# Cached decode attention, two branches: 20 of 128 token slots of each value tile weighted by ScalarE and summed by VectorE, outputs gathered two groups at a time

## The chip, the cores and the metric

The kernel runs on one core of one Trainium2 chip. The metric is the device time of one execution in microseconds (us); the verdict on a change is taken between runs of both kernels on the same chip.

## What is computed

Two attention branches A and B each answer one new token per batch entry (2 of them) against a cache of 4096 tokens, 32 heads, head size 128, all in float32. Their outputs are mixed by a gate:

```python
q = (x @ wq).reshape(B, 1, 32, 128).transpose(0, 2, 1, 3)
scores = einsum("bhqd,bhkd->bhqk", q, k_cache) * 128 ** -0.5
p = softmax(scores, axis=-1)
o = einsum("bhqk,bhkd->bhqd", p, v_cache)
branch = o.transpose(0, 2, 1, 3).reshape(B, 1, 4096) @ wo
g = sigmoid((A_x * gate_w).sum(-1, keepdims=True))
out = g * branch_A + (1 - g) * branch_B      # both branches are fed A_x
```

The four caches are 134.2 MB each (2 x 32 x 4096 x 128 x 4 bytes), the four weight matrices 8.4 MB each. Every byte is used once, so some 570 MB have to be read from HBM.

## The kernel before

The work is cut into 32 **units** (`units`, `NU`): branch n, group g of four heads, batch entry b. A unit's keys fill one tile `kt` of 128 partitions x 128 token slots x 128 values (8.4 MB), and its values one tile `vt` of the same size. Each of the four heads has a quarter of the partitions, 32 of them, and a partition holds 128 consecutive tokens, the **slots**. There are two key buffers (`kpool`, also used for `wq` and `wo`) and one value buffer (`vpool`).

All big loads go out on SyncE's one queue, in the order of a list written out by hand (`order`): wq of A, wq of B, the keys of unit 0, and then the keys of unit u+1 and the values of unit u, in turn; at the end wo of A, the values of unit 31 (three pieces) and wo of B (six pieces). `pump` issues the next load of the list once the buffer that it needs has been given free by `used`; on the chip SyncE waits at each load for the last reader of that buffer. So the values of unit u are issued after the last value product of unit u-1 (the buffer is the same one), and the keys of unit u+2 after the scores of unit u.

The schedule is manual: each engine runs its instructions as the program writes them. The loop over u (at the end of the function) handles the keys of unit u and the values of unit v = u-1 together:

- `scores(u, k)`, four chunks of 32 slots: VectorE multiplies the chunk in place by the query (L232, TENSOR_TENSOR) and sums each slot over its 128 values (L233, TENSOR_REDUCE into `sc`). Chunks 0 and 1 stand before `values(v)` in the program, chunks 2 and 3 behind it, but `values(v)` is work of TensorE alone.
- `values(v)`: 32 products (L258), each of four slots: the weights `padded` (128 x 32) against 128 x 512 of `vt`, into `vp` in PSUM. A product shows as two MATMUL records in the trace, 64 for a unit. GpSimd then clears the weights (L261).
- `take_out` and `gather_out`, every second unit, when both batch entries of a group are in: ScalarE (L275) and VectorE (L281, three times) fold the four slot columns of `vp` into `vs`, and a product with `pick` (L285) places them in `heads`.
- `soft(u)`: maximum over slots and partitions (L241, L244, L246 on VectorE), then ScalarE's four exponentials, one per head, straight into `padded` (L249), each with its row sum into `lp`.
- `sum_of(n)` and `deal_out(n)`, once per branch: the row sums become `rs`, and eight products with the table `deal` (L294) turn `heads` into `on`, the layout that the product with wo wants (`project_out`, L307, and `project_last`, L318).

## Time and profile before

| | |
|---|---|
| median of three runs | 1326.93 us (1326.4 to 1327.3) |
| the profiled execution | 1326.39 us |
| its span, first to last instruction | 1324.6 us |
| VectorE (DVE) busy | 1181.6 us, 89% |
| TensorE (PE) busy | 356.9 us, 27% |
| ScalarE (ACT) busy | 74.6 us, 6% |
| read from HBM | 570.43 MB, 431 GB/s over the span |

Busy times are shares of the whole span. In the rows below DVE is VectorE, PE TensorE, ACT ScalarE, SPq SyncE's queue. A row of a timeline has start and length in us; in brackets stand the idle time before it and what ended that.

### The profile page before, as it was taken

The numbers are of one execution on the slowest core, as the hardware profiler recorded it, in microseconds if no ns is written. First come the engines' busy times: TensorE is split into PE (matmuls) and PEld (weight loads), VectorE is DVE, ScalarE is ACT, GpSimd is POOL, SyncE is SP. The second block draws the span as 40 slices with busy tenths as digits, with TensorE's granted clock in tenths as the row PEclk, the third lists the DMA queues.
The fourth block names the chain that finished last, engine by engine and source line by source line (L and its number), as shares of the span: only waits on it lengthen the run. The fifth ranks groups of instructions, "written<-read, shape, count | busy, mean of one in ns | idle before, by whom it ended". The sixth has DMA issues, their size and how long they took to land.

```text
span 1324.6 us, 5989 instructions
## 1 busy us (share of the span) xinstructions
PE 356.9 (27%) x2406; PEld 104.7 (8%) x2406; DVE 1181.6 (89%) x477; ACT 74.6 (6%) x285; POOL 18.0 (1%) x40
## 2 busy tenths in 40 slices
PE   3202322211232221123233022232202222220257
PEld 0000000000000000000001000000000000000012
DVE  2499999999999999999999999999999999999960
ACT  0000000000000000000000000000000000000000
POOL 0000000000000000000000000000000000000000
PEclk9656666556666655666665566666556666656667
DMA  9999999999999999999999999999999999999998
GB/s 412 442 436 422 440 441 418 439 440 430 433 434 439 426 431 441 434 435 426 441 430 432 440 426 440 433 434 429 440 437 422 440 439 426 431 442 439 418 431 346
DMA packets 11130, 570.83 MB, mean 431 GB/s; under 512 B 1239, under 2 KB 1243, under 8 KB 1630
## 3 DMA queue, kind: packets, MB, share of 16 engines
q1 hardware_dynamic: 11092, 570.43, 99.5%
q8 instruction: 19, 0.31, 0.1%
q14 instruction: 9, 0.07, 0.0%
q10 hardware_dynamic: 10, 0.01, 0.0%
HBM read 570.43 MB, written 0.00 MB: 431 GB/s over the span
## 4 chain that ended last, share of the span: by engine, by line
DMA 76%; PE 23%; issue 0%; DVE 0%; SPq 0%; ACT 0%
DMA vt<-in_A_v_cache_dram 37%; DMA vt<-in_B_v_cache_dram 35%; PE vp L258 22%; DMA kt<-in_B_wq_dram 3%; DMA kt<-in_B_wo_dram 2%; PE qa L209 1%; DVE kt L215 0%; SPq L62 0%; ACT kt L214 0%; PE qa L318 0%; ACT kt L376 0%; DVE qcolB L217 0%
## 5 line engine op out<-in xcount | busy, mean ns | idle before, releaser
L232 DVE TENSOR_TENSOR kt<-kt,q 128x4096 f32<-128x4096 f32 x128 | 565.5, 4418 | 46.2 <-DMA kt<-in_B_k_cache_dram 28.9
L233 DVE TENSOR_REDUCE sc<-kt 128x32 f32<-128x4096 f32 x128 | 565.7, 4420 | 6.5
L258 PE MATMUL vp<-vt,pr 128*32 128x512 f32 x2048 | 298.9, 749 | 797.4 <-DMA vt<-in_A_v_cache_dram 424.2
L258 PEld LDWEIGHTS vp<-vt,pr 128*32 128x32 f32 x2048 | 81.8, 134 | 1005.2 <-issue 1000.5
L249 ACT ACTIVATE pr<-sc,nm 32x128 f32<-32x128 f32 x128 | 50.9, 398 | 723.7 <-DVE nm L246 721.3
L285 PE MATMUL heads<-vs,pick 128*128 128x128 f32 x32 | 12.4, 491 | 124.2 <-DVE vs L281 124.2
L261 POOL MEMSET pr<- 128x512 f32 x32 | 16.8, 524 | 1268.0 <-PE vp L258 1230.1
L275 ACT ACTIVATE vs<-vp,slot 128x128 f32<-128x128 f32 x16 | 5.9, 368 | 451.0 <-PE vp L258 451.0
L281 DVE SCALAR_TENSOR_TENSOR vs<-vp,slot,vs 128x128 f32<-128x128 f32 x48 | 16.7, 348 | 13.5 <-ACT vs L275 12.4
L209 PE MATMUL qa<-kt,cols 128*2 128x512 f32 x128 | 18.3, 728 | 22.1 <-DMA kt<-in_B_wq_dram 15.8
L249 ACT ACTIVATION_READ_ACCUMULATOR pr<-sc,nm 32x1 f32 x128 | 23.5, 184 | 0.0
L215 DVE STREAM_TRANSPOSE kt<-kt 128x1024 f32<-128x1024 f32 x1 | 1.2, 1245 | 21.8 <-ACT kt L214 21.8
L307 PE MATMUL most<-kt,on 128*2 128x512 f32 x120 | 17.3, 734 | 11.1 <-DMA kt<-in_A_wo_dram 10.7
L285 PEld LDWEIGHTS heads<-vs,pick 128*128 128x128 f32 x32 | 7.8, 304 | 138.8 <-DVE vs L281 138.8
L378 DVE COPY kt<-qa 2x128 f32<-2x128 f32 x2 | 0.6, 280 | 14.6 <-PE qa L318 14.6
L337 DVE TENSOR_REDUCE kt<-kt 128x32 f32<-128x128 f32 x1 | 0.4, 378 | 13.7 <-POOL kt masks.py:199 13.7
L215 DVE STREAM_TRANSPOSE vt<-vt 128x1024 f32<-128x1024 f32 x1 | 1.2, 1245 | 10.0 <-ACT vt L214 10.0
L241 DVE TENSOR_REDUCE rm<-sc 128x1 f32<-128x128 f32 x32 | 9.0, 281 | 0.6
L244 DVE STREAM_TRANSPOSE q<-rm 128x32 f32<-128x32 f32 x32 | 6.8, 211 | 1.1
L294 PE MATMUL small<-vs,deal 128*128 128x32 f32 x32 | 7.2, 402 | 0.9 <-ACT vs L290 0.9
L294 PEld LDWEIGHTS small<-vs,deal 128*128 128x128 f32 x32 | 7.0, 330 | 1.4 <-ACT vs L290 1.4
L146 DVE COPY cols<-small 128x8 f32<-128x8 f32 x1 | 0.2, 167 | 7.6 <-PE small L144 7.6
(53 smaller groups left out, 44.0 us busy)
## 6 DMA issues: line engine op xcount, KB each, us to landing
kt<-in_A_wq_dram SPq DMA_DIRECT2D x2, 4096.0 KB, 16.6
kt<-in_A_k_cache_dram SPq DMA_DIRECT2D x2, 4096.0 KB, 31.2
vt<-in_B_v_cache_dram SPq DMA_DIRECT2D x1, 4096.0 KB, 20.2
kt<-in_B_wo_dram SPq DMA_DIRECT2D x1, 4096.0 KB, 33.4
vt<-in_B_v_cache_dram SPq DMA_DIRECT2D x1, 3072.0 KB
kt<-in_B_wo_dram SPq DMA_DIRECT2D x1, 2048.0 KB
...
```

Source lines behind the costliest of these rows:

```text
L209: nc.tensor.matmul(t[h * QT:h * QT + B], cols[:, c], halves[:, c, i, h], start=c == 0, stop=c == KC - 1)
L232: nc.vector.tensor_tensor(t, t, qs[u][:, None, :].to_broadcast([P, NH, DH]), op=ALU.mult)
L233: nc.vector.tensor_reduce(sc[u][:, k * NH:(k + 1) * NH], t, axis=AX.X, op=ALU.add)
L241: nc.vector.tensor_reduce(rm, sc[u], axis=AX.X, op=ALU.max)
L244: nc.vector.transpose(across, rm.to_broadcast([P, PH]))
L249: nc.scalar.activation(padded[h, :, b, j * VC:(j + 1) * VC], sc[u][h].rearrange("p (c a) -> p c a", a=VC), AF.Exp, bias=nm[h], accum_out=l ...
L258: nc.tensor.matmul(vp[n, g][s * QT:(s + 1) * QT], padded[:, c].rearrange("p b m -> p (b m)"), vt[u][:, c * VC:(c + 1) * VC].rearrange("p a ...
L261: nc.gpsimd.memset(padded[:, :, b], 0.0)
L281: nc.vector.scalar_tensor_tensor(t, vp[n, g][:, a * DH:(a + 1) * DH], slot[:, a:a + 1], t, op0=ALU.mult, op1=ALU.add)
L285: nc.tensor.matmul(heads[n], pick[:, (NG - g) * B:][:, :P], t, start=g == 0, stop=g == NG - 1)
L294: nc.tensor.matmul(dealt[:, b], deal[:, b, k].rearrange("p g h q -> p (g h q)"), t[:, k * OR:(k + 1) * OR], start=k == 0, stop=k == DQ - 1)
L307: nc.tensor.matmul(most[s * QT:s * QT + B], on[n][:, r], wo[n][:, r], start=n == "A" and r < STRIPS, stop=n == "B" and r >= EARLY - STRIPS)
```

## The change

1. **Values.** Slots 0 to 19 of the value tile no longer go through five products. `weigh`: ScalarE multiplies each of the 20 slots by its probability, in place (20 ACTIVATEs of 128 x 128). `add_up`: VectorE adds the five blocks of four slots into the first with three TENSOR_TENSORs (1024, 512 and 512 elements per partition). `values_added`: one product with a constant table `plain` takes the sum. So a unit has 27 + 1 products in place of 32.
2. **Order.** `scores(u, 2)` moves between `values` and `add_up`, so on VectorE the three additions stand between the third and the fourth chunk. The value buffer is given free after `values_added`.
3. **Scores.** In chunk 0, the sums of 12 of the 32 slots go from VectorE to ScalarE (12 ACTIVATEs with an accumulated sum); VectorE's first reduction is left with 20 slots.
4. **Softmax.** One exponential over 128 partitions into `pc`, with its row sum into `ls`, then four copies into `padded` (27 blocks of 4 slots in place of 32).
5. **Outputs.** `vs` holds two groups; every fourth unit one product of 256 columns places both (`gather_out`). `sum_of` sums with two small products in place of a transpose and a reduction; `deal_out` turns the outputs with three VectorE transposes in place of eight products, and the table `deal` goes.
6. **Start.** wq of A is loaded by one DMA in place of two.

```diff
+ADDED = 5
+NA = ADDED * VC
+NP = NVC - ADDED
+HELP = 12
-        load(t, ins[n + "_wq"].rearrange("(p c) f -> p c f", c=KC), *((0, KC // 2, KC) if n == "A" else (0, KC)))
+        load(t, ins[n + "_wq"].rearrange("(p c) f -> p c f", c=KC), 0, KC)
...
     def scores(u, k):
...
-        nc.vector.tensor_reduce(sc[u][:, k * NH:(k + 1) * NH], t, axis=AX.X, op=ALU.add)
+
+        n = HELP if k == 0 else 0
+        for r in range(n):
+            nc.scalar.activation(t[:, r], t[:, r], AF.Copy, accum_out=sc[u][:, r:r + 1])
+        nc.vector.tensor_reduce(sc[u][:, k * NH + n:(k + 1) * NH], t[:, n:], axis=AX.X, op=ALU.add)
...
+        pc[u] = small.tile([P, NS], F32, name="pc")
+        nc.scalar.activation(pc[u], sc[u], AF.Exp, bias=nm, accum_out=ls[:, g % N2, g // N2, b:b + 1])
         for j, h in enumerate(QUARTERS):
-            nc.scalar.activation(padded[h, :, b, j * VC:(j + 1) * VC], sc[u][h].rearrange("p (c a) -> p c a", a=VC),
-                                 AF.Exp, bias=nm[h], accum_out=lp[h, g * B + b:g * B + b + 1])
+            nc.scalar.activation(padded[h, :, b, j * VC:(j + 1) * VC],
+                                 pc[u][h, NA:].rearrange("p (c a) -> p c a", a=VC), AF.Copy)
+
+    def weigh(u):
+
+        for r in range(NA):
+            nc.scalar.activation(vt[u][:, r], vt[u][:, r], AF.Copy, scale=pc[u][:, r:r + 1])
+
+    def add_up(u):
+
+        t = vt[u][:, :NA].rearrange("p (c a) d -> p c (a d)", a=VC)
+        nc.vector.tensor_tensor(t[:, 0:2], t[:, 0:2], t[:, 2:4], op=ALU.add)
+        nc.vector.tensor_tensor(t[:, 0], t[:, 0], t[:, 1], op=ALU.add)
+        nc.vector.tensor_tensor(t[:, 0], t[:, 0], t[:, 4], op=ALU.add)
...
-        for c in range(NVC):
...
+        for i in range(NP):
+            value_product(u, i, padded[:, i], NA + i * VC)
         nc.gpsimd.memset(padded[:, :, b], 0.0)
 
+    def values_added(u):
+        value_product(u, NP, plain[:, units[u][2]], 0)
...
+    def gather_out(n, y):
+
+        if y == 0:
+            heads[n] = ps.tile([P, N2, DH], F32, name="heads", bufs=1)
+        nc.tensor.matmul(heads[n].rearrange("p i d -> p (i d)"), pick[:, P - (y + 1) * QT:][:, :P],
+                         vs[n, y].rearrange("p i d -> p (i d)"), start=y == 0, stop=y == NG // N2 - 1)
...
+        for k in range(N2):
+            nc.scalar.activation(even[:, k], heads[n][:, k], AF.Copy, scale=rs[n][:, k:k + 1])
+
+        turned = small.tile([P, N2, DQ, QT], F32, name="turned")
+        nc.vector.transpose(turned.rearrange("p i q m -> p (i q m)"), even.rearrange("p i d -> p (i d)"))
+        on[n] = small.tile([P, B, OR], F32, name="on")
         for b in range(B):
-            for k in range(DQ):
-                nc.tensor.matmul(dealt[:, b], deal[:, b, k].rearrange("p g h q -> p (g h q)"), t[:, k * OR:(k + 1) * OR],
-                                 start=k == 0, stop=k == DQ - 1)
...
+            nc.vector.transpose(on[n][:, b], turned[:, :, :, :GB].rearrange("p i q (h b) -> p b i h q", b=B)[:, b])
...
         if v >= 0:
+            weigh(v)
             values(v)
+        if u < NU:
+            scores(u, 2)
+        if v >= 0:
+            add_up(v)
+            values_added(v)
             used("v", v)
         if ends:
             take_out(*ends)
         if u < NU:
-            scores(u, 2)
             scores(u, 3)
             used("k", u)
```

How the instructions stand now, at three places. In these rows a name is output<-inputs, `vt` a value tile, `kt` a key tile, and the brackets name the engines and loads whose count the instruction waits for.

VectorE in the loop's pass u = 1, before: the four chunks, each a multiplication and a reduction, and behind them the maximum.

```order
L232 TENSOR_TENSOR kt_210<-kt_210,q_237 128x4096 [waits DMAHW7_49,DVE_49,PE_49]
L233 TENSOR_REDUCE sc_239<-kt_210 128x32 [waits DVE_49,Activation_49]
L232 TENSOR_TENSOR kt_210<-kt_210,q_237 128x4096
L233 TENSOR_REDUCE sc_239<-kt_210 128x32 [waits DVE_49]
L232 TENSOR_TENSOR kt_210<-kt_210,q_237 128x4096
L233 TENSOR_REDUCE sc_239<-kt_210 128x32 [waits DVE_49]
L232 TENSOR_TENSOR kt_210<-kt_210,q_237 128x4096
L233 TENSOR_REDUCE sc_239<-kt_210 128x32 [waits DVE_49]
L241 TENSOR_REDUCE rm_286<-sc_239 128x1 [waits DVE_49]
```

The same pass now:

```order
L243 TENSOR_TENSOR kt_213<-kt_213,q_254 128x4096 [waits DMAHW6_49,DVE_49,PE_49]
L248 TENSOR_REDUCE sc_256<-kt_213 128x20 [waits DVE_49,Activation_49]
L243 TENSOR_TENSOR kt_213<-kt_213,q_254 128x4096
L248 TENSOR_REDUCE sc_256<-kt_213 128x32 [waits DVE_49]
L243 TENSOR_TENSOR kt_213<-kt_213,q_254 128x4096
L248 TENSOR_REDUCE sc_256<-kt_213 128x32 [waits DVE_49]
L277 TENSOR_TENSOR vt_215<-vt_215 128x1024 [waits DMAHW2_49,DMAHW7_49,DMAHW0_49,Activation_49]
L278 TENSOR_TENSOR vt_215<-vt_215 128x512 [waits DVE_49]
L279 TENSOR_TENSOR vt_215<-vt_215 128x512 [waits DVE_49,Activation_49]
L243 TENSOR_TENSOR kt_213<-kt_213,q_254 128x4096
L248 TENSOR_REDUCE sc_256<-kt_213 128x32 [waits DVE_49]
L256 TENSOR_REDUCE rm_334<-sc_256 128x1 [waits DVE_49]
```

The first reduction has shrunk to 20 slots, and three additions on the value tile, which wait for ScalarE, stand ahead of the fourth chunk. The first reduction of the pass before, u = 0, waits for nothing but VectorE:

```order
L243 TENSOR_TENSOR kt_169<-kt_169,q_217 128x4096 [waits DMAHW4_49,DMAHW1_49,DVE_49]
L248 TENSOR_REDUCE sc_219<-kt_169 128x20 [waits DVE_49]
L243 TENSOR_TENSOR kt_169<-kt_169,q_217 128x4096
L248 TENSOR_REDUCE sc_219<-kt_169 128x32 [waits DVE_49]
L243 TENSOR_TENSOR kt_169<-kt_169,q_217 128x4096 [waits DMAHW5_49]
```

TensorE at the end, before: the last unit's products, the gather, the eight products with `deal`, and the product with wo of B.

```order
L258 MATMUL vp<-vt,pr 32x512 [waits DMAHW0_49]
L258 MATMUL vp<-vt,pr 32x512 x3
L285 MATMUL heads<-vs,pick 128x128 [waits DVE_49]
L294 MATMUL small<-vs,deal 128x32 [waits Activation_49]
L294 MATMUL small<-vs,deal 128x32 x7
L307 MATMUL most<-kt,on 2x512 [waits DMAHW1_49,Activation_49]
```

And now:

```order
L285 MATMUL vp<-vt,pr 32x512 [waits DMAHW7_49]
L285 MATMUL vp<-vt,pr 32x512 x3
L285 MATMUL vp<-vt,plain 32x512 [waits DVE_49]
L327 MATMUL heads<-vs,pick 128x256 [waits DVE_49]
L350 MATMUL most<-kt,on 2x512 [waits DMAHW0_49,DVE_49]
```

The products with `deal` are gone; the product with wo waits for VectorE's transposes instead of ScalarE's copy.

## Rows read from the trace of the kernel before

**Rows 1.** The page: SyncE's DMA queue, packets, MB, share of 16 engines.
```profile
q1 hardware_dynamic: 11092, 570.43, 99.5%
```
**Rows 2.** The page: the chain that ended last, by engine.
```profile
DMA 76%; PE 23%; issue 0%; DVE 0%; SPq 0%; ACT 0%
```
**Rows 3.** Windows: stretch, length, busy (count) of PE, PEld, DVE, ACT, POOL; PEclk, DMA share, GB/s.
```profile
4.00:43.00 39.00, 11.96 (x78) 3.02 (x82) 8.91 (x31) 1.36 (x3) 0.00 (x0) 0.85 0.99 430
...
101.00:1262.00 1161.00, 295.25 (x1966) 87.75 (x1966) 1103.97 (x412) 64.77 (x257) 15.73 (x30) 0.61 1.00 434
```
**Rows 4.** The chain in order of time: start, length, what.
```profile
53.16 47.77 DMA vt<-in_A_v_cache_dram
...
101.07 9.80 PE vp L258 x64
110.89 28.66 DMA vt<-in_A_v_cache_dram
...
265.12 29.26 DMA vt<-in_A_v_cache_dram
...
1233.64 28.43 DMA vt<-in_B_v_cache_dram
...
1291.95 29.41 DMA kt<-in_B_wo_dram
...
1321.40 0.47 PE qa L318 x8
```
**Rows 5.** VectorE's timeline: first multiplication of passes 1, 2, 3 and 6.
```profile
89.37 4.43 DVE L232 TENSOR_TENSOR kt<-kt,q 128x4096 f32<-128x4096 f32 x1
...
125.85 4.43 DVE L232 TENSOR_TENSOR kt<-kt,q 128x4096 f32<-128x4096 f32 x1
...
163.23 4.42 DVE L232 TENSOR_TENSOR kt<-kt,q 128x4096 f32<-128x4096 f32 x1
...
275.18 4.43 DVE L232 TENSOR_TENSOR kt<-kt,q 128x4096 f32<-128x4096 f32 x1 [1.67 <-DMA kt<-in_A_k_cache_dram]
```
**Rows 6.** Groups by line and form, VectorE: xcount | busy us, mean ns | idle before, releasers.
```profile
L233 DVE TENSOR_REDUCE sc<-kt 128x32 f32<-128x4096 f32 x128 | 565.7, 4420 | 6.5
L232 DVE TENSOR_TENSOR kt<-kt,q 128x4096 f32<-128x4096 f32 x128 | 565.5, 4418 | 46.2 <-DMA kt<-in_B_k_cache_dram 28.9 <-DMA kt<-in_A_k_cache_dram 17.0
...
L223 DVE STREAM_TRANSPOSE q<-qcolB 128x128 f32<-128x128 f32 x16 | 5.0, 312 | 0.6
...
L148 DVE TENSOR_TENSOR vt<-cols,small 128x8 f32<-128x8 f32 x1 | 0.2, 168 | 0.0
```
**Rows 7.** The same of ScalarE.
```profile
L249 ACT ACTIVATE pr<-sc,nm 32x128 f32<-32x128 f32 x128 | 50.9, 398 | 723.7 <-DVE nm L246 721.3
L249 ACT ACTIVATION_READ_ACCUMULATOR pr<-sc,nm 32x1 f32 x128 | 23.5, 184 | 0.0
L275 ACT ACTIVATE vs<-vp,slot 128x128 f32<-128x128 f32 x16 | 5.9, 368 | 451.0 <-PE vp L258 451.0
```
**Rows 8.** Timeline of the start: issues of the first loads, the two query projections.
```profile
0.74 0.87 SPq L62 DMA_DIRECT2D kt<-in_A_wq_dram  x2
...
16.30 9.76 PE L209 MATMUL qa<-kt,cols 128*2 128x512 f32 x64 [6.22 <-DVE qa L205]
...
26.12 26.93 SPq L62 DMA_DIRECT2D kt<-in_A_k_cache_dram  x3
...
41.85 8.64 PE L209 MATMUL qa<-kt,cols 128*2 128x512 f32 x64 [15.78 <-DMA kt<-in_B_wq_dram]
```
**Rows 9.** TensorE's timeline at the end.
```profile
1307.32 0.49 PE L285 MATMUL heads<-vs,pick 128*128 128x128 f32 x2 [1.66 <-DVE vs L281]
1308.27 3.62 PE L294 MATMUL small<-vs,deal 128*128 128x32 f32 x16 [0.46 <-ACT vs L290]
1312.20 7.74 PE L307 MATMUL most<-kt,on 128*2 128x512 f32 x56 [0.31 <-ACT on L297]
1320.11 0.62 PE L318 MATMUL qa<-kt,on 128*2 128x128 f32 x16 [0.17 <-DMA kt<-in_B_wo_dram]
```

More of the change, by code (lines that the diff above doesn't have):

```diff
@@ L138, in tile_gated_decode @@
     make_identity(nc, ident)
-    ones = start(1)
+    ones = small.tile([P, 1], F32, name="ones")
     nc.vector.memset(ones, 1.0)
@@ L161, in tile_gated_decode @@
     nc.vector.tensor_scalar(gate["B"], gate["A"], -1.0, 1.0, op0=ALU.mult, op1=ALU.add)
-    padded = small.tile([P, NVC, B, G * VC], F32, name="pr")
+    padded = small.tile([P, NP, B, G * VC], F32, name="pr")
     nc.vector.memset(padded, 0.0)
-    lp = small.tile([P, PH], F32, name="lp")
+    plain = small.tile([P, B, B, G * VC], F32, name="plain")
+    nc.vector.memset(plain, 0.0)
+    for b in range(B):
+        for j, h in enumerate(QUARTERS):
+            nc.vector.memset(plain[h, b, b, j * VC:(j + 1) * VC], 1.0)
+    lp = small.tile([P, N2, NG // N2, QT], F32, name="lp")
     nc.vector.memset(lp, 1.0)
+    ls = small.tile([P, N2, NG // N2, B], F32, name="ls")
+    quarter = small.tile([P, G], F32, name="quarter")
+    nc.vector.tensor_reduce(quarter, ident.rearrange("p (h m) -> p h m", h=G), axis=AX.X, op=ALU.add)
     slot = small.tile([P, VC], F32, name="slot")
     nc.vector.tensor_reduce(slot, ident.rearrange("p (m a) -> p a m", a=VC), axis=AX.X, op=ALU.add)
-    pick = small.tile([P, NG * B + P], F32, name="pick")
+    pick = small.tile([P, P - QT + P], F32, name="pick")
     nc.vector.memset(pick, 0.0)
@@ L182, in tile_gated_decode @@
             ident.rearrange("p (s b h a) -> p s b h a", s=STRIPS, b=B, a=VC)[:, :, b], axis=AX.X, op=ALU.add)
-        nc.vector.tensor_reduce(pick[:, NG * B + b:][:, :P - QT + 1:QT], more, axis=AX.X, op=ALU.add)
-    deal = small.tile([P, B, DQ, NG, G, DQ], F32, name="deal")
-    nc.vector.memset(deal, 0.0)
-    for b in range(B):
-        for k in range(DQ):
-            nc.vector.tensor_copy(deal[:, b, k, :, :, k],
-                                  ident.rearrange("p (h g b) -> p b g h", h=G, b=B)[:, b, :NG])
-    small.tile([P, 56], F32, name="gap")
+        nc.vector.tensor_reduce(pick[:, P - QT:P - QT + GB].rearrange("p (h b) -> p h b", b=B)[:, :, b], more,
+                                axis=AX.X, op=ALU.add)
+    small.tile([P, 72], F32, name="gap")
     qcol = {}
@@ L255, in values, with sum_slots @@
             vp[n, g] = ps.tile([P, VC * DH], F32, name="vp", bufs=2)
-        for c in range(NVC):
-            s = c % STRIPS
-            nc.tensor.matmul(vp[n, g][s * QT:(s + 1) * QT], padded[:, c].rearrange("p b m -> p (b m)"),
-                             vt[u][:, c * VC:(c + 1) * VC].rearrange("p a d -> p (a d)"),
-                             start=b == 0 and c < STRIPS, stop=b == B - 1 and c >= NVC - STRIPS)
+        for i in range(NP):
+            value_product(u, i, padded[:, i], NA + i * VC)
         nc.gpsimd.memset(padded[:, :, b], 0.0)
+    def values_added(u):
+        value_product(u, NP, plain[:, units[u][2]], 0)
     def sum_of(n):
-        across = across_heads()
-        nc.vector.transpose(across, lp)
-        rs[n] = small.tile([P, 1], F32, name="rs")
-        nc.vector.tensor_reduce(rs[n], across, axis=AX.X, op=ALU.add)
-        nc.vector.reciprocal(rs[n], rs[n])
-        nc.vector.tensor_tensor(rs[n], rs[n], gate[n], op=ALU.mult)
-    def take_out(n, g):
-        vs[n, g] = small.tile([P, DH], F32, name="vs")
-        nc.scalar.activation(vs[n, g], vp[n, g][:, :DH], AF.Copy, scale=slot[:, :1])
-    def gather_out(n, g):
-        t = vs[n, g]
+        total = ps.tile([P, N2], F32, name="small", bufs=1)
+        for h in range(G):
+            nc.vector.tensor_scalar(lp[:, :, :, h * B:(h + 1) * B], ls, quarter[:, h:h + 1], None, op0=ALU.mult)
+        for i in range(N2):
+            nc.tensor.matmul(total[:, i:i + 1], lp[:, i].rearrange("p y m -> p (y m)"), ones, start=True, stop=True)
+        rs[n] = small.tile([P, N2], F32, name="rs")
+        nc.vector.reciprocal(rs[n], total)
+        nc.vector.tensor_tensor(rs[n], rs[n], gate[n].to_broadcast([P, N2]), op=ALU.mult)
+    def take_out(n, g):
+        if g % N2 == 0:
+            vs[n, g // N2] = small.tile([P, N2, DH], F32, name="vs")
+        nc.scalar.activation(vs[n, g // N2][:, g % N2], vp[n, g][:, :DH], AF.Copy, scale=slot[:, :1])
+    def sum_slots(n, g):
+        t = vs[n, g // N2][:, g % N2]
         for a in range(1, VC):
@@ L317, in project_last @@
             for t, e in strips():
-                nc.tensor.matmul(t, on["B"][:, r], wo["B"][:, r, e], start=r == EARLY, stop=r == OR - 1)
+                nc.tensor.matmul(t, on["B"][:, :, r], wo["B"][:, r, e], start=r == EARLY, stop=r == OR - 1)
     for n in "AB":
@@ L348, in tile_gated_decode @@
         if ends:
-            gather_out(*ends)
+            n, g = ends
+            sum_slots(n, g)
+            if g % N2 == N2 - 1:
+                gather_out(n, g // N2)
         if u == NU // 2:
```

22 lines of the change are left out of this document (11 added, 11 removed).

## The prediction

> **What bounds the kernel now.** I read first how full the transfers are, then the chain, then the loop's rhythm, and last the engine that is nearly as full as the transfers.
>
> SyncE's queue moves 570.43 MB and keeps the sixteen DMA engines busy for 99.5% of the span [rows 1]. In the middle of the run the DMA share is 1.00 at 434 GB/s, and at the start, where VectorE is busy for 8.91 of 39 us, it is 0.99 at 430 GB/s [rows 3]: the rate doesn't depend on whether the engines work. At 434 GB/s the bytes alone need 1314.4 us of the span of 1324.6 us, so no change to the computing can win more than 10 us.
>
> The chain gives TensorE 23% [rows 2], which reads as if the value products stood on the path. In order of time it alternates between a value load and a unit's products, 9.80 us in the first one [rows 4]. But a value load takes 28 to 29 us from its issue (28.66, 29.26) while its 8.4 MB need 19.3 us at 434 GB/s: it waits some 9 to 10 us in the queue behind a key load. The products end before that key load does, so they are covered. The values of unit 0 landed at 53.16 + 47.77 = 100.93, those of unit 30 at 1233.64 + 28.43 = 1262.07 [rows 4]: 30 units, **38.70 us each**. The keys land midway between two value tiles: in pass 6 VectorE waits for them until 275.18 [rows 5], and that pass's value tile lands at 265.12 + 29.26 = 294.38 [rows 4], 19.2 us later.
>
> VectorE takes 125.85 - 89.37 = 36.48 us for pass 1 and 163.23 - 125.85 = 37.38 us for pass 2, which folds a group [rows 5], 36.93 on average: 1.77 us less than the transfers give it. That shows as the 46 us that it waits for keys [rows 6]. So the bound is the transfers, VectorE second with 95% (1103.97 of 1161 us), ScalarE nearly idle (64.77 us) [rows 3].
>
> **The change part by part.**
>
> *VectorE, each pass.* Gone: 12 of 128 slots' sums, 12/32 x 4.42 = 1.66 us [rows 6]. New: three additions of 1024, 512 and 512 elements. A TENSOR_TENSOR of 4096 takes 4418 ns, one of 8 takes 168 ns [rows 6], so 1.04 ns an element and 0.16 us fixed: 1.22 + 0.69 + 0.69 = 2.60 us. In proportion to the large row alone it would be 2.21 us, with a whole small row on top of each 2.71; I take 2.60, since the fit passes through both rows. With 0.1 us for hand-overs a pass takes 36.93 - 1.66 + 2.70 = **38.0 us**, 0.7 less than the transfers. Cover is left, but thin: 0.7 us in place of 1.77.
>
> *ScalarE, each pass.* Weighing 20 rows of 128 x 128 with a scale from a tile: the same form from PSUM takes 368 ns [rows 7], so 7.4 us; 8.0 at the 398 ns of the exponentials. The 12 sums cost at most 398 + 184 ns each [rows 7], 7.0 us, from the end of the first multiplication (4.4 us after the keys land) to 11.4; the values land at 19.3. The softmax's copies replace exponentials of like size. Some 17 of 38.7 us: ScalarE has the time.
>
> *The wait that the change adds.* The additions wait for the weighing, and behind them on VectorE stand the fourth chunk and the softmax. Weighing ends 19.3 + 0.1 + 7.4 = 26.8 us after the keys landed; VectorE gets to the additions after three chunks, 3 x 8.84 - 1.66 = 24.9 us after it starts the pass. Starting on time it waits 1.9 us and ends the pass 1.2 us late (2.1 where a group is folded); starting late by that much it waits no longer. So its lag behind the keys settles between 1 and 2.5 us and doesn't add up.
>
> *The value buffer's release.* It moves from the end of the products (19.3 + 0.1 + 9.8 = 29.2 us after the keys landed) to the last product behind the additions: at most 27.4 + 2.7 + 0.3 = 30.4, while the next key load runs until 38.7. SyncE sends the next value load 8 us before the queue runs out. The key buffer's release lags with VectorE; behind it the value load's 19.3 us are still to run.
>
> *The first passes* are the tightest. VectorE starts late there, since the second projection lies ahead of its scores: pass 1 at 89.37 [rows 5], now 1.66 us sooner, 87.7, with keys that landed at 100.93 - 19.3 = 81.6, a lag of 6.1 us. The additions then run from 112.6 to 115.3, the last product to 115.6, and the value load goes out there in place of 110.89 [rows 4]. The key load ahead of it ends midway between 100.93 and 139.55, at 120.2: 4.6 us of cover, down from 9.3. From there the lag shrinks by 0.7 us a pass. The branch's end at pass 16 puts copies, products and transposes on VectorE's way, by the rows some 3 us once, at a time when the lag is under 2.5: less than in pass 1.
>
> *Start.* wq of A comes in one piece. Its products, 9.76 us, now begin after the whole 8.4 MB, at about 21 us, and end by 31; the key load that waits for them goes out then instead of at 26.12, while wq of B is in transit until 41.85 [rows 8]. Cost nothing. The two pieces leave no hole today: 0.99 busy from 4 us on [rows 3]. The Trainium skill ("SBUF — State Buffer", section on the DMA setup-cost knee) says that every transfer pays a roughly fixed 2 us whatever its size. By that rule one piece instead of two would save 2 us and the sum would be 1324.8; the row of full DMA engines speaks against it for queued loads.
>
> *End.* Out: the eight products with the table, 3.62 us, and 0.3 us for the copy behind them [rows 9]. In: one more value product (0.3), a gather of twice the columns (0.49 more at most), a second ScalarE copy (0.37), three transposes (at most 2 x 0.31, 0.31 and 0.31, by the 312 ns of 128 x 128 [rows 6]), 2.4 us together. The product with wo starts 1.5 us sooner. But the last piece of wo lands at 1291.95 + 29.41 = 1321.36, and only 0.47 us of products follow [rows 4]; TensorE waits 0.17 us for a piece ahead of that [rows 9]. So this gains nothing, or at most some tenths.
>
> *Sum.* Start 0, loop 0, end 0 to -0.3: the profiled execution's 1326.39 stays as it is. The median of the runs is 0.5 above that execution, so I write **1326.8 us**: no change, where 0.2% (2.65 us) is about what a measurement of this kernel can tell from none.
>
> The rule table of the Trainium skill's page "ScalarE: Activation LUTs" ("Rules for kernel authors") sends multiplications to VectorE, not ScalarE. Followed here, the 20 weighings would stand on the engine with 0.7 us to spare, and the loop would slow by many times that; the windows' shares, 95% and 6%, speak for the change's choice.
>
> **The rivals.**
>
> *TensorE was on the path* (faster). The chain names it, and four of 32 products go, 9.80/8 = 1.2 us a unit, 38 us in all; the transfers would stop that at 10, so 1316. Against it: the DMA share of 1.00, the 9 us that each value load spends in the queue, and that the buffer's release doesn't come sooner at all. 4 in 100 with all else that could be faster.
>
> *VectorE becomes the bound* (slower). The additions stand on the engine with 0.7 us to spare. If a pass takes longer than 38.8 us, that is if the additions cost 3.4 us or more rather than 2.6, the lag grows in each of 31 passes, eats the 4.6 us of cover (less what an issue needs to start) and from then on the queue runs empty once a unit. At 3.9 us a pass is 39.3, 31 x 0.6 - 4.6 = 14 us: 1340. At the far bound, all three as dear as one row of 4096, 4.42 us, it is 31 x 1.1 - 4.6 = 30 us: 1356. For it: the margin is a fiftieth of a pass, and ScalarE now works beside VectorE in the same tiles, which no row shows. Against it: both rows of this operation agree on 2.2 to 2.7. 5 in 100.
>
> *The change doesn't take the sums off VectorE* (slower). If the shortened first reduction had to wait for ScalarE's 12 sums in the same tile, each pass would gain up to 7 us: 45 us a pass, 31 x 6.3 - 4.6 = 191 us, 1517. In the order of instructions it waits for a ScalarE count in later passes, as it did before; in pass 0 it waits for VectorE alone, so the wait should be that for the old exponential. 2 in 100.
>
> **How the numbers follow.** No change 0.89, faster 0.04, slower 0.07. The forecast's own spread is that of the runs shown (0.9 us from lowest to highest) with some tenths at the end and up to 2 us for a start that goes otherwise than I think: 1324.6 to 1329.4. That leaves out the rivals, 1 in 10 together, and the 2 in 10 allowed need no more.
>
> **What would show it.** Right: the DMA share stays 1.00 and a unit 38.70 us; VectorE is busy for 37 to 38 us a pass, hardly waits for keys, and waits up to 2 us for ScalarE ahead of the additions; these cost 2.5 to 2.8 us; the second value load goes out near 115.6 us; the weighing takes 6 to 8 us; the last wait is for wo. Wrong: a unit over 38.8 us with holes in the DMA rows behind value loads that go out late; a first reduction that waits for ScalarE's sums; or a span under 1321 us, which would mean that the transfers had room that the rows don't show.

## The result and the profile after

The changed kernel is slower by 0.4%: 1331.7 us (1331.6 to 1332.7) against 1326.8 us, ratio 1.0038, 95% interval 1.0027 to 1.0048. That is 4.9 us, and outside the range given. The profiled execution (1332.7 us, span 1330.9) is 6.3 us longer than the one of before; it is the slowest of the six, the other five took 1331.6 to 1332.0 us.

First the page of the changed kernel: the busy line, the DMA queues, the chain by engine.

```profile
PE 347.7 (26%) x2110; PEld 90.8 (7%) x2110; DVE 1212.4 (91%) x584; ACT 371.4 (28%) x1629; POOL 15.9 (1%) x40
...
q1 hardware_dynamic: 10948, 570.43, 99.1%
q8 instruction: 16, 0.26, 0.1%
q14 instruction: 22, 0.18, 0.0%
...
DVE 49%; DMA 40%; issue 7%; PE 4%; ACT 0%; DVEq 0%; SPq 0%; ACTq 0%
```

Transfers are less full than in [rows 1], and the chain has moved from TensorE to VectorE. One line matters more than it looks: the queue q14, kind "instruction". The page of before has 9 packets of 8 KB there, this one 22:

```profile
q14 instruction: 9, 0.07, 0.0%
```

The groups of the new work in the changed kernel, columns as in [rows 6]:

```profile
L243 DVE TENSOR_TENSOR kt<-kt,q 128x4096 f32<-128x4096 f32 x128 | 565.6, 4418 | 17.6 <-DMA kt<-in_B_k_cache_dram 11.2
...
L272 ACT ACTIVATE vt<-vt,pc 128x128 f32<-128x128 f32 x640 | 190.6, 388 | 328.5 <-DMA vt<-in_B_v_cache_dram 170.9
L247 ACT ACTIVATE kt<-kt 128x128 f32<-128x128 f32 x384 | 112.7, 294 | 114.6 <-DVE kt L243 114.6
...
L247 ACT ACTIVATION_READ_ACCUMULATOR kt<-kt 128x1 f32 x384 | 71.6, 186 | 0.0
L285 PE MATMUL vp<-vt,plain 128*32 128x512 f32 x64 | 36.9, 660 | 32.1 <-DVE vt L279 31.9
L277 DVE TENSOR_TENSOR vt<-vt 128x1024 f32<-128x1024 f32 x32 | 38.9, 1216 | 3.5 <-ACT vt L272 3.5
...
L279 DVE TENSOR_TENSOR vt<-vt 128x512 f32<-128x512 f32 x32 | 22.1, 692 | 3.3
```

The additions cost what the sum had, 1.22 + 0.69 + 0.69 us. They wait for ScalarE once in the whole run, for 3.5 us in the last unit, when VectorE has no chunk left to do:

```profile
1302.66 1.23 DVE L277 TENSOR_TENSOR vt<-vt 128x1024 f32<-128x1024 f32 x1 [3.49 <-ACT vt L272]
```

VectorE waits 17.6 us for keys where it waited 46 [rows 6]. So the computing behaves; where are the 6.3 us? The windows (columns as in [rows 3]) of the loop, and of pass 1:

```profile
101.00:1262.00 1161.00, 288.68 (x1698) 76.80 (x1698) 1126.26 (x506) 343.02 (x1517) 13.74 (x30) 0.61 1.00 433
...
114.00:116.00 2.00, 0.00 (x0) 0.00 (x0) 1.97 (x3) 0.00 (x0) 0.00 (x0) 0.50 0.38 164
116.00:118.00 2.00, 0.65 (x1) 0.18 (x2) 1.90 (x3) 0.00 (x0) 0.00 (x0) 0.50 1.24 528
118.00:120.00 2.00, 1.26 (x2) 0.00 (x0) 2.00 (x1) 0.00 (x0) 0.00 (x0) 0.50 0.00 0
120.00:122.00 2.00, 0.00 (x0) 0.00 (x0) 1.97 (x2) 0.00 (x0) 0.00 (x0) 0.50 1.53 524
```

A window counts a packet where it starts. From 118 to 120 us none starts: of the key load's last sixteen 64 KB packets twelve are through between 118.5 and 118.9 us, and the value load's first start at 120.25. It is a **hole** of up to 1.8 us (and the first sixteen packets behind it take 3.1 us at the median in place of 2.4). The timelines of VectorE, TensorE and SyncE say whose it is:

```profile
89.72 4.43 DVE L243 TENSOR_TENSOR kt<-kt,q 128x4096 f32<-128x4096 f32 x1
114.56 1.22 DVE L277 TENSOR_TENSOR vt<-vt 128x1024 f32<-128x1024 f32 x1
116.60 0.69 DVE L279 TENSOR_TENSOR vt<-vt 128x512 f32<-128x512 f32 x1
```
```profile
117.35 1.92 PE L285 MATMUL vp<-vt,plain 128*32 128x512 f32 x2 [7.21 <-DVE vt L279]
```
```profile
119.30 0.33 SPq L68 DMA_DIRECT2D vt<-in_A_v_cache_dram  x1
```

The last value product frees the buffer at 119.27 us, and the load goes out at 119.30; before, it went out right after the products' end at 110.87 [rows 4].

The second place is the end. Windows of the last microseconds, first of the kernel before, then of the changed one:

```profile
1320.00:1321.00 1.00, 0.89 (x30) 0.63 (x32) 0.00 (x0) 0.60 (x1) 0.00 (x0) 1.00 0.11 43
1321.00:1322.00 1.00, 0.68 (x20) 0.11 (x8) 0.16 (x1) 0.10 (x1) 0.00 (x0) 1.00 0.07 16
```
```profile
1324.00:1325.00 1.00, 1.00 (x12) 0.08 (x4) 0.00 (x0) 0.00 (x0) 0.00 (x0) 1.00 0.06 25
1325.00:1326.00 1.00, 0.86 (x11) 0.11 (x8) 0.00 (x0) 0.00 (x0) 0.00 (x0) 1.00 0.07 27
1326.00:1327.00 1.00, 0.83 (x24) 0.41 (x24) 0.00 (x0) 0.60 (x1) 0.00 (x0) 1.00 0.06 25
```

A share of 0.06 is one DMA engine in sixteen. In the changed kernel **one of them works alone for 3 us** while all others are done. A load leaves sixteen landing marks in the trace, read here as one for each DMA engine, and a tile has landed with the last. For the last load of wo:

| kernel | first mark | second-last | last | last - first |
|---|---|---|---|---|
| before | 1316.87 | 1321.07 | 1321.36 | 4.49 |
| changed | 1320.13 | 1324.22 | 1327.58 | 7.45 |
| e1_two_pieces | 1319.25 | 1322.91 | 1326.54 | 7.29 |
| e2_early_add | 1319.16 | 1323.14 | 1325.65 | 6.49 |
| e3_few_act | 1317.91 | 1321.85 | 1322.12 | 4.21 |
| e5_few_act_early | 1317.47 | 1320.83 | 1321.36 | 3.89 |
| e12_outputs_aligned | 1316.81 | 1320.99 | 1321.08 | 4.27 |
| e13_idle_ops_aligned | 1317.93 | 1321.44 | 1324.49 | 6.56 |
| e14_shift_32_bytes | 1319.95 | 1324.62 | 1324.87 | 4.92 |
| e16_idle_ops_split | 1317.04 | 1321.22 | 1321.53 | 4.49 |

The 6.22 us of the last mark split in two: 3.26 that every engine is late (0.16 before the hole, 2.55 at the value load behind it, 3.1 by unit 5, hardly more after that), and 2.96 by which the last one falls behind the first.

### The profile page after: what moved, and what is told of

It is laid out like the page before. It is cut to its first block, busy times and chain, and to the rows that moved or that the text cites. A ratio compares the mean times of both kernels' runs of the same rounds, so it can differ in the third digit from the quotient of the medians.

```text
span 1330.9 us, 6993 instructions
## 1 busy us (share of the span) xinstructions
PE 347.7 (26%) x2110; PEld 90.8 (7%) x2110; DVE 1212.4 (91%) x584; ACT 371.4 (28%) x1629; POOL 15.9 (1%) x40
## 4 chain that ended last, share of the span: by engine, by line
DVE 49%; DMA 40%; issue 7%; PE 4%; ACT 0%; DVEq 0%; SPq 0%; ACTq 0%
DVE kt L243 26%; DVE sc L248 18%; DMA kt<-in_B_k_cache_dram 12%; DMA kt<-in_A_k_cache_dram 12%; DMA vt<-in_B_v_cache_dram 10%; DMA kt<-in_B_wq_dram 3%; PE vp L285 3%; DMA kt<-in_B_wo_dram 2%; DVE vt L277 2%; DVE vt L278 1%; DVE vt L279 1%; PE qa L220 1%; DVE vs L320 0%; DVE q L234 0%; DVE rm L256 0%
## 5 line engine op out<-in xcount | busy, mean ns | idle before, releaser
L243 DVE TENSOR_TENSOR kt<-kt,q 128x4096 f32<-128x4096 f32 x128 | 565.6, 4418 | 17.6 <-DMA kt<-in_B_k_cache_dram 11.2
L248 DVE TENSOR_REDUCE sc<-kt 128x32 f32<-128x4096 f32 (+1 forms) x128 | 514.6, 4020 | 6.5
L285 PE MATMUL vp<-vt,pr 128*32 128x512 f32 x1728 | 269.3, 772 | 838.6 <-DMA vt<-in_A_v_cache_dram 439.0
L272 ACT ACTIVATE vt<-vt,pc 128x128 f32<-128x128 f32 x640 | 190.6, 388 | 328.5 <-DMA vt<-in_B_v_cache_dram 170.9
L247 ACT ACTIVATE kt<-kt 128x128 f32<-128x128 f32 x384 | 112.7, 294 | 114.6 <-DVE kt L243 114.6
L247 ACT ACTIVATION_READ_ACCUMULATOR kt<-kt 128x1 f32 x384 | 71.6, 186 | 0.0
L285 PE MATMUL vp<-vt,plain 128*32 128x512 f32 x64 | 36.9, 660 | 32.1 <-DVE vt L279 31.9
L277 DVE TENSOR_TENSOR vt<-vt 128x1024 f32<-128x1024 f32 x32 | 38.9, 1216 | 3.5 <-ACT vt L272 3.5
L266 ACT ACTIVATE pr<-pc 32x108 f32<-32x108 f32 x128 | 37.2, 290 | 4.0 <-ACT pc L264 0.4
L295 POOL MEMSET pr<- 128x432 f32 x32 | 14.7, 458 | 1277.7 <-PE vp L285 1168.8
L279 DVE TENSOR_TENSOR vt<-vt 128x512 f32<-128x512 f32 x32 | 22.1, 692 | 3.3
L278 DVE TENSOR_TENSOR vt<-vt 128x512 f32<-128x512 f32 x32 | 22.2, 692 | 1.1
```

What stands on the lines that cost most here:

```text
L243: nc.vector.tensor_tensor(t, t, qs[u][:, None, :].to_broadcast([P, NH, DH]), op=ALU.mult)
L247: nc.scalar.activation(t[:, r], t[:, r], AF.Copy, accum_out=sc[u][:, r:r + 1])
L248: nc.vector.tensor_reduce(sc[u][:, k * NH + n:(k + 1) * NH], t[:, n:], axis=AX.X, op=ALU.add)
L266: nc.scalar.activation(padded[h, :, b, j * VC:(j + 1) * VC], pc[u][h, NA:].rearrange("p (c a) -> p c a", a=VC), AF.Copy)
L272: nc.scalar.activation(vt[u][:, r], vt[u][:, r], AF.Copy, scale=pc[u][:, r:r + 1])
L277: nc.vector.tensor_tensor(t[:, 0:2], t[:, 0:2], t[:, 2:4], op=ALU.add)
```

## The experiments

The first theory was the hole, and its rival that something takes time from the DMA engines all along. The kernel before had 1326.5 to 1326.7 us beside each of these runs.

### The start and the hole

e1 loads wq of A in two pieces again:

```diff
-        load(t, ins[n + "_wq"].rearrange("(p c) f -> p c f", c=KC), 0, KC)
+        load(t, ins[n + "_wq"].rearrange("(p c) f -> p c f", c=KC), *((0, KC // 2, KC) if n == "A" else (0, KC)))
```

> The changed kernel with the first weight load (wq of A) again in two pieces. Theory 1, the empty queue: in pass 1 the value buffer comes free so late that the queue runs dry; VectorE starts pass 1 at 89.72 us, 1.9 us of it because the start is later (54.79 against 52.91 us). With the old start the second value load goes out at about 117.4 instead of 119.30 us and most of the hole closes: 1329.9 to 1330.7 us, from 1331.7. Theory 2, instruction loads: ScalarE's longer program (1629 instructions against 285) is loaded through the DMA engines that carry the data, and holds one of them up; the start has nothing to do with it, at most the 0.5 us by which the first weights land later come back: 1331.2 us. Theory 3, VectorE is the bound in every pass: 1331.2 to 1331.7 us.

Measured 1331.86 us, ratio 1.0039 (1.0026 to 1.0051). e2 puts the additions ahead of the third chunk in passes 1 to 5:

```diff
+        early = 0 < u <= 5
-        if u < NU:
+        if u < NU and not early:
             scores(u, 2)
...
+            if early:
+                scores(u, 2)
             scores(u, 3)
```

> The changed kernel with the additions and the last value product ahead of the third chunk of scores in passes 1 to 5 alone, so that the value buffer comes free some 7 us sooner where VectorE is late; the passes after that are as before. Theory 1, the empty queue: the value tiles of units 1 to 4 lost 2.6 us against the kernel before; they come back: 1329.1 us (1328.7 to 1329.9). Theory 2, instruction loads alone: nothing changes in the number of instructions, 1331.7 us. Theory 3, VectorE the bound in every pass: it has the same work, 1331.7 us.

Measured 1331.89 us, 1.0036 (1.0024 to 1.0049). Neither gains what the first theory expected; both stand within 0.2 us of the rivals' times. The marks say why: the hole **moved**. In e2 all engines are on time (0.1 us) up to pass 6, the first with the old order; the value tile of unit 6 is 1.7 us late, and from unit 9 on it is 2.3 us. SyncE's timeline of e2 there:

```profile
264.46 0.33 SPq L68 DMA_DIRECT2D vt<-in_A_v_cache_dram  x1
280.93 0.33 SPq L68 DMA_DIRECT2D kt<-in_A_k_cache_dram  x1
311.64 0.33 SPq L68 DMA_DIRECT2D vt<-in_A_v_cache_dram  x1
318.46 0.33 SPq L68 DMA_DIRECT2D kt<-in_A_k_cache_dram  x1
```

Between the two value loads lie 47.2 us where a unit has 38.6: the second waits for additions that stand behind the third chunk again. In e1 1.2 us are lost by unit 5 and 1.1 more between 738 and 758 us, behind VectorE's work for the end of branch A (702.7 to 706.7 us); the changed kernel, 3.1 us late by then, loses nothing there. So most of what is not lost in the first hole is lost in a later one. And in both the one slow DMA engine stays.

### ScalarE's number of instructions

e3 does ScalarE's work on the 32 rows of a pass in three instructions. It leaves out the sums of the 12 slots and the separate weights of the 20: one weight serves all.

```diff
-        for r in range(n):
-            nc.scalar.activation(t[:, r], t[:, r], AF.Copy, accum_out=sc[u][:, r:r + 1])
+        if n:
+            nc.scalar.activation(t[:, :n].rearrange("p r d -> p (r d)"), t[:, :n].rearrange("p r d -> p (r d)"), AF.Copy)
+            nc.scalar.activation(sc[u][:, :n], t[:, :n, 0], AF.Copy)
...
-        for r in range(NA):
-            nc.scalar.activation(vt[u][:, r], vt[u][:, r], AF.Copy, scale=pc[u][:, r:r + 1])
+        t = vt[u][:, :NA].rearrange("p r d -> p (r d)")
+        nc.scalar.activation(t, t, AF.Copy, scale=pc[u][:, :1])
```

> The changed kernel with ScalarE's 32 rows of each pass handled by 3 instructions in place of 32 (and 12 reads of the accumulator): one copy over the 12 slots, one that writes their 12 scores, one copy over the 20 value slots with a single scale. Left out: the sums of 12 of 128 slots and the separate weights of 20; the same elements are read and written. Theory 2, instruction loads: ScalarE's program is about as long as before the change, the instruction packets on q14 fall from 22 to about 12, and the 3 us by which one DMA engine ends later are gone: 1328.7 us (1328 to 1329.5). Theory 1, the empty queue alone: the additions come no sooner in pass 1, 1331.7 us. Theory 4, ScalarE's traffic in the tiles slows the transfers: the traffic is the same, 1331.7 us.

Measured 1327.58 us, 1.0008 (0.9999 to 1.0017), below the 1328 to 1329.5 expected: 4.1 of the 4.9 us are gone, with VectorE's and TensorE's work as it was. The first mark is 1.04 us late in place of 3.26, and the spread to 4.21. The page of e3:

```profile
PE 350.1 (26%) x2110; PEld 91.2 (7%) x2110; DVE 1212.4 (91%) x584; ACT 197.3 (15%) x317; POOL 15.8 (1%) x40
...
q14 instruction: 10, 0.08, 0.0%
```

ScalarE is also busy for 197 us in place of 371, so e3 alone doesn't tell the number of its instructions from their time; the idle instructions further down do.

e5 is e3 with the edits of e1 and e2; it leaves out the same.

> The changed kernel with three things undone together: ScalarE's rows in 3 instructions a pass (as in e3_few_act; left out: the sums of 12 of 128 slots and the separate weights of 20), the additions ahead of the third chunk in passes 1 to 5 (as in e2_early_add), and the first weights in two pieces. After the first four runs: e3 alone took 4.1 of the 4.9 us away, e1 and e2 nothing. Instruction loads (theory 2) with the empty queue as a small second cost: the 0.9 us that e3 had left over the kernel before go too, 1326.7 us. Instruction loads alone, with the rest from elsewhere (VectorE's additions, the 27 + 1 products): 1327.6 us as e3.

Measured 1326.75 us, 1.0002 (0.9994 to 1.0011). So start and hole are worth some 0.8 us once ScalarE's program is short; the single runs of e3 and e5 overlap, so this figure is a rough one.

### Idle instructions

If the instructions themselves cost time, idle ones in the kernel before must do it too. e4 adds 42 a pass on ScalarE, which brings its count to the 1629 of the changed kernel, e6 42 on GpSimd, e4b 84 on ScalarE:

```diff
+    idle = small.tile([P, 2], F32, name="idle")
+    nc.vector.memset(idle, 0.0)
...
+            for _ in range(42):
+                nc.scalar.activation(idle[:, 1:2], idle[:, :1], AF.Copy)
```

> The kernel before with 42 more ScalarE instructions in each pass (copies of one element per partition on a tile of their own, that nothing waits for): 1344 in all, the number that the change adds. Theory 2, instruction loads: the instruction packets on q14 go from 9 to about 20, one DMA engine ends some 3 us later, 1329.8 us (1328.5 to 1331) from 1326.8. Theories 1, 3 and 4: nothing is added to VectorE, to the buffers' release or to the traffic in the tiles, 1326.8 us.

> The kernel before with 42 more GpSimd instructions in each pass (MEMSETs of one element per partition that nothing waits for), 1344 in all, where e4_act_idle_ops had ScalarE's. Theory 2 in general, any engine's instructions come through the DMA engines: q14's packets go from 9 to about 19 again and the run takes 1329.5 to 1334 us. Theory 2 for ScalarE's alone (its loads meet a DMA engine that is already last, GpSimd's meet another with room): packets as many, but 1326.8 to 1327.5 us.

> The kernel before with 84 more ScalarE instructions in each pass, twice those of e4_act_idle_ops. e4 took 7.2 us more than the kernel before: its value tiles landed 0.1 us later each from the first on (38.72 against 38.60 us a unit, and packets of 2421 ns in place of 2418), some 3.5 us over the run, and some came 0.65 us later still. If all of it comes from the number of instructions, twice as many give 14 us: 1341 us. If the slower packets have another cause in that program, and only the instruction loads double: 1326.8 + 3.5 + 7.4 = 1337.7 us, or 1334 us where the packets take 2418 ns. If a saturation sets in (the one engine that is held up is the same), between 1334 and 1337.

Measured: e4 1333.93 us (1.0054), e6 1332.32 (1.0044), e4b 1342.34 (1.0120; 1.0104 to 1.0135). The packets on q14: 19, 19 and 30. So 2688 instructions that nothing waits for cost 15.7 us. But e4 stands 3 us above its range, since the runs hid a second effect: their 64 KB data packets took 2421 ns at the median, from the first cache loads on, where before, the changed kernel and e1 to e5 have 2418.

### The outputs alone, and a control

e7 is the changed kernel without weighing, additions and help with the sums (`ADDED = 0`, `HELP = 0`, old order); e8 is e7 with wq of A in two pieces; e9 is e7 with `HELP = 12`; e10 and e11 are e4 with 21 and with 1 idle instruction.

> The changed kernel without its first three parts: all 32 products, all sums on VectorE, the order of the chunks as before; what stays is the gather of two groups, the softmax through a copy, the sums by two products and the outputs by transposes, and the first weights in one piece. Theory 2: ScalarE's program is about as long as before, so no loss, 1326.3 to 1327.2 us. A rival, that the outputs' part or the start costs a share of the 4.9 us: 1328 us or more. The end's chain is 1.5 us shorter by my working, but the last load is what it waits for, so no gain over some tenths.

> The kernel of e7_outputs_only (outputs gathered two groups at a time, no weighing, no help from ScalarE; 1329.1 us) with the first query weights loaded in two pieces again. If e7's 2.4 us over the kernel before came from the start in one piece (later first loads, or 16 transfer engines that stand otherwise to each other from then on), this comes back to 1326.5 to 1327.2, with packets of 2418 ns. If the 2.4 us come with the packets of 2421 ns whatever the start, it stays at 1328.8 to 1329.4.

> The changed kernel with ADDED = 0: ScalarE takes 12 rows of the first score chunk (384 instructions more than e7_outputs_only), but weighs no slots, VectorE adds nothing up and no value product waits. The theory that each further 8 KB of instructions holds up one transfer engine by 0.65 us expects 3 more packets on the instruction queue than e7 and 1 to 2 us more than a kernel with the same time per packet: 1327.7 to 1328.7 with packets of 2418 ns, 1330 to 1331 with 2421 ns. The rival that the 4.9 us come with the weighing and the late value product expects no more than e7: 1329.1 or below.

> The kernel before with 21 idle ScalarE instructions a pass, half of e4_act_idle_ops (1333.9 us, 7.2 above the kernel before). The theory that the time goes with the bytes of instructions expects half the packets more on the instruction queue (about 14) and 2.5 to 3.6 us: 1329.2 to 1330.3. The rival that part of e4's 7.2 us is a fixed price of the idle tile or of the rebuilt program (packets of 2421 ns) expects 1331 to 1332.

> The kernel before with 1 idle ScalarE instruction a pass (32 in all, a quarter of an 8 KB packet): a control. The theory of instruction bytes expects 1326.6 to 1327.0 and packets of 2418 ns. The rival, that any rebuilt program with its buffers at other places gets packets of 2421 ns, expects 1328.5 to 1329.2.

Measured: e7 1329.11 us (1.0020), e8 1329.11 (1.0019), e9 1330.43 (1.0028), e10 1330.53 (1.0028), e11 1329.88 (1.0024; 1.0015 to 1.0034). The control is the surprise: 32 idle instructions cost 3.3 us, and 640 more only 0.65. All five have packets of 2421 or 2422 ns in the loop. What they share is where the big tiles lie: small tiles stand ahead of them, and a new or a smaller one moves them all. Before, changed, e1, e2, e3, e5: from byte 28160 of a partition on. e4, e4b, e6, e10, e11: 28192. e7, e8, e9: 28800.

### Place and instructions apart

The padding tile `gap` sets that place. e14 is the kernel before with 8 numbers more in it and nothing else:

```diff
-    small.tile([P, 56], F32, name="gap")
+    small.tile([P, 64], F32, name="gap")
```

e12 is e8, e13 e4, e15 e9, each with `gap` cut so that the tiles start at 28672, 28160 and 28672.

> The kernel before with its padding tile grown from 56 to 64 numbers and nothing else: the same instructions, all landing buffers 32 bytes further. The theory of place expects 2421 ns a packet and what e11 had, 1329.2 to 1330.1 us. The rival, that the 3 us of e11 came with its 32 instructions, expects 1326.3 to 1327.0.

> e8_outputs_two_pieces (1329.1 us) with the padding tile cut from 72 to 40 numbers, so that the landing buffers start at byte 28672 of a partition, a multiple of 512. The theory that the place of the buffers sets the packets' time expects 2418 ns and 1326.2 to 1327.0 us: the new way of gathering outputs costs nothing. The rival, that gathering outputs itself costs 2.5 us (or that only byte 28160 is good), expects 1328.8 to 1329.4.

> e4_act_idle_ops (42 idle ScalarE instructions a pass, 1333.9 us) with the padding tile cut from 56 to 48 numbers, so that the buffers stand where they stood before. The theory of two separate causes expects 2418 ns a packet and the difference between e4 and e11 alone on top of the kernel before: 1326.6 + 4.05 = 1330.7, from 1330.0 to 1331.5. If place is nothing, it stays at 1333.5 to 1334.3; if instructions are nothing, it falls to 1326.6 to 1327.2.

> e9_help_only (outputs, and ScalarE's help with 12 rows of the scores; 1330.4 us) with the buffers at byte 28672. It should lie above e12_outputs_aligned by what e9 lay above e7 and e8, 1.3 us: 1327.5 to 1328.5. Then the weighing's 640 further ScalarE instructions and the late value product are worth the rest up to the changed kernel, 3.2 to 4.2 us. If help costs nothing, it stands at 1326.2 to 1327.0.

Measured:

| | us | ratio, 95% | packet, median |
|---|---|---|---|
| e14, shift by 32 bytes alone | 1329.89 | 1.0025 (1.0015 to 1.0034) | 2421 ns |
| e12, outputs alone | 1326.79 | 1.0000 (0.9992 to 1.0009) | 2418 ns |
| e15, and help with the sums | 1327.30 | 1.0005 (0.9996 to 1.0014) | 2418 ns |
| e13, 1344 idle ScalarE instructions | 1329.70 | 1.0023 (1.0013 to 1.0032) | 2418 ns |

e14 and e12 fell as expected; e13 lies 0.3 us and e15 0.2 us below its range. The place costs 3.2 us with the same instructions; the changed kernel doesn't pay it. 28160 and 28672 are multiples of 256 bytes (of 512 too), 28192 and 28800 are not. The Trainium skill ("DMA: Bandwidth & Descriptors", section on how a descriptor splits into AXI transactions) says that a transaction must start from a 256B-aligned address, and of a descriptor that doesn't start on one that "the bytes before the start are fetched but unused and still cost beats". It says so of what is read; here the side written to has moved, and the four places agree with a step of 256 bytes. But the place alone doesn't decide: in e14 the 64 KB packets of wq of B, whose tile has moved by 32 bytes too, still take 2418 ns, and only those of the caches 2421. The windows of the loop show it in one digit, e14 with the instructions of before:

```profile
101.00:1262.00 1161.00, 293.81 (x1966) 87.25 (x1966) 1101.23 (x411) 64.76 (x257) 15.76 (x30) 0.61 1.00 433
```

against 434 GB/s in [rows 3]. Instructions cost 3.0 us in e13, gathering outputs nothing, help with the sums and the start in one piece 0.5 us (e15 less e12; their intervals overlap).

### One engine's instructions or everybody's

e13's 1344 instructions cost 3.0 us, the 704 that ScalarE has more in e15 than before 0.6. Nor is it ScalarE alone: e6, with 1344 on GpSimd, stands 2.4 us over e14, whose place it has. e16 is e13 with 21 idle instructions on ScalarE and 21 on GpSimd a pass, so with the same bytes:

```diff
-    small.tile([P, 48], F32, name="gap")
+    small.tile([P, 40], F32, name="gap")
...
+    blank = small.tile([P, 2], F32, name="blank")
...
-            for _ in range(42):
+            for _ in range(21):
                 nc.scalar.activation(idle[:, 1:2], idle[:, :1], AF.Copy)
+                nc.gpsimd.memset(blank, 0.0)
```

> The kernel of e13_idle_ops_aligned (42 idle ScalarE instructions a pass, 1329.7 us), with 21 of them on ScalarE and 21 on GpSimd: the same bytes of instructions, buffers at the same place. If each engine's instructions come through a transfer engine of their own that has slack for some 5 packets before it is the last, this costs 0 to 0.8 us: 1326.6 to 1327.4, and no transfer engine stands alone at the end. If only the sum of the bytes counts, it stays with e13: 1329.3 to 1330.1.

Measured 1326.56 us, 1.0001 (0.9992 to 1.0010): **nothing**. Page and end windows of e16, then the end windows of e13:

```profile
PE 352.1 (27%) x2406; PEld 102.8 (8%) x2406; DVE 1181.7 (89%) x478; ACT 210.8 (16%) x957; POOL 82.6 (6%) x712
...
q14 instruction: 19, 0.16, 0.0%
```
```profile
1321.00:1322.00 1.00, 0.71 (x32) 0.53 (x24) 0.00 (x0) 0.37 (x1) 0.00 (x0) 1.00 0.10 23
1322.00:1323.00 1.00, 0.26 (x12) 0.00 (x0) 0.56 (x2) 0.54 (x2) 0.00 (x0) 1.00 0.00 0
```
```profile
1322.00:1323.00 1.00, 1.00 (x16) 0.20 (x8) 0.00 (x0) 0.00 (x0) 0.00 (x0) 1.00 0.06 25
1323.00:1324.00 1.00, 0.89 (x20) 0.32 (x16) 0.00 (x0) 0.60 (x1) 0.00 (x0) 1.00 0.06 25
```

Both load 19 packets of instructions. In e13 one DMA engine is still at work alone in 1323 to 1324 us; in e16 none is after 1322. So ScalarE's and GpSimd's packets seem to burden different DMA engines, each of which has time for some five more before it is the last; which engine carries a packet the trace doesn't name.

e17 is the changed kernel with e1's start and the weighing as one GpSimd product, 20 instructions a pass less:

```diff
-        for r in range(NA):
-            nc.scalar.activation(vt[u][:, r], vt[u][:, r], AF.Copy, scale=pc[u][:, r:r + 1])
+        t = vt[u][:, :NA]
+        nc.gpsimd.tensor_tensor(t, t, pc[u][:, :NA, None].to_broadcast([P, NA, DH]), op=ALU.mult)
```

> The changed kernel with the first query weights in two pieces and the 20 slots weighed by one GpSimd product (weights broadcast along the slot) instead of 20 ScalarE instructions; sums, plain product and all outputs as in the changed kernel. The theory of instruction bytes expects 6 or 7 packets less on the instruction queue than the changed kernel (15 or 16) and the time of e15 or a little over, 1327.0 to 1328.5. The rival, that the weighing and its late value product cost the 4.4 us, expects 1330.5 to 1332. A third way: GpSimd slows VectorE beside it; where VectorE's pass of 38.0 us grows by more than 0.6, VectorE bounds the loop, with 32 us more for each us over.

Measured 1345.26 us (1339.8 to 1349.8), 1.0139: the third way. Packets fell to 15 and the spread at the end to 2.9 us, but VectorE's multiplication, 4411 to 4426 ns in every pass of the changed kernel, now takes up to 8625:

```profile
L243 DVE TENSOR_TENSOR kt<-kt,q x128: 4414/4417/8625, 53.1 to 1288.8; 128x4096 f32<-128x4096 f32 x128
...
L272 POOL TENSOR_TENSOR vt<-vt,pc x32: 4462/5402/8587, 101.3 to 1310.1; 128x2560 f32<-128x2560 f32 x32
```

(minimum, median, maximum.) Most are untouched, and where two meet, one stands for about the other's length. The Trainium skill ("SBUF — State Buffer", section on its two separate sides) says that a VectorE instruction with two inputs in SBUF and a GpSimd one that reads SBUF block each other fully; the maxima agree, each a little under both lengths together (4417 + 4462 = 8879). The reductions, with one input, stay at 4020 ns on average as in the changed kernel. So e17 did not separate the weighing's instructions from its late product.

## Why the prediction was wrong

The forecast was no change, 1324.6 to 1329.4 us; the kernel came out 4.9 us slower. By its steps:

- **Bound, VectorE's additions, waits, end: right.** Units that nothing disturbs take 38.60 us in both kernels (the 38.70 holds what the last DMA engine falls behind). The additions cost 2.60 us; they wait for ScalarE in no pass but the last, where up to 2 us in each were allowed; VectorE's pass grew by (1126.26 - 1103.97)/30 = 0.74 us, where 1.07 was expected. The weighing takes 5.97 us for 20 rows back to back, not 7.4. The end waits for wo and then 0.47 us of products, as before. e12 shows that outputs and softmax copies cost nothing.
- **"ScalarE, each pass ... ScalarE has the time": the step that failed.** It counted 1344 added instructions as time on an idle engine. The term that is missing is what they add to the transfers. Instructions that aren't TensorE's number 5989 - 2 x 2406 = 1177 before and 2773 after; 13 packets more for 1596 more, about 123 in 8 KB. From e10 to e4, both at the same place, 672 instructions and 5 packets cost 3.4 us: some 0.7 us a packet, estimated. In e16 and e15 the first 5 or 6 packets cost next to nothing; a likely reason is that their DMA engine has time left, since before the engines end up to 4.49 us apart. Those behind make it the last. e13 has 10 packets more and pays 3.0 us. The changed kernel's trace shows such a lag too, the 2.96 us; from unit 10 on nine of 21 units take 39.1 to 39.5 us, mostly 39.28, instead of 38.60, and an 8 KB packet lies in each of those (two further units have one and take 38.60). By itself a packet takes 0.31 us; why it sets its engine back by 0.68 isn't shown. The page of before had the line; its share of 0.0% is of sixteen engines, while nine times 0.68 is 6 us of a single one.
- **"The first passes": mis-sized.** The last product takes 1.92 us there, not 0.3. Pass 1 starts at 89.72, not 87.7, since the second projection began 0.5 us later and took 9.98 us where it took 8.64 [rows 8]. So the load goes out at 119.30, 3.7 us later than the 115.6 reckoned. And the cover was less: the packets of the key load run out from 118.5 us on, not at 120.2, where the tile of keys has landed with its last mark, and the first packet starts 0.95 us after the issue. That is 118.5 - 0.95 - 115.6 = 1.9 us of cover in place of 4.6, and 3.7 - 1.9 is the hole of 1.8. The sum had the mechanism and said that pass 1 was the tightest. "From there the lag shrinks" held too weakly for e1 and e2 to win: their holes came later.
- **"Start. Cost nothing".** Right: two pieces or one, 1331.86 against 1331.7, and 1329.11 in both e8 and e7. The 2 us of the Trainium skill's page "SBUF — State Buffer" (DMA setup-cost knee) aren't seen for loads in a queue, as the sum had it.
- **The rivals**, TensorE on the path, VectorE as the bound and sums that stay on it, did not come true.

Shown are 3.0 us for the number of instructions (e13, in the kernel before) and 0.9 us for all else with few instructions (e3). About 1 us of the 4.9 is left, and its cause stays open. In the traces all engines are late by 3.3 us in the changed kernel and by 1.04 in e3. The end of the weighing isn't why: in pass 1 of the changed kernel it is over at 107.51 us, and the additions start at 114.56, right behind VectorE's third chunk. VectorE starts that pass at 89.72 us there and at 88.02 in e3, because TensorE's second projection ran at a lower granted clock in the execution that was traced. The windows around it, first of the changed kernel, then of e3 (columns as in [rows 3]):

```profile
42.00:52.40 10.40, 9.98 (x64) 1.83 (x64) 0.00 (x0) 0.60 (x1) 0.00 (x0) 0.70 1.02 440
```
```profile
42.00:52.40 10.40, 8.31 (x64) 1.63 (x64) 1.30 (x2) 1.19 (x2) 0.00 (x0) 0.87 1.04 446
```

So most of the 1.7 us by which pass 1 starts later come from the clock in that execution, the slowest of the six, and how large the hole is in the other five isn't known. Why the place costs 3.2 us, when 512 packets of 64 KB on each engine at 4.5 ns more (the means are 2419.5 and 2424.0) make 2.3 and the smaller ones 0.3, isn't settled either. No version tried beats the kernel before; the intervals of e3, e5, e12, e15 and e16 include no change.
